# Reordering one turn of an RWKV-6 and mixture-of-depths kernel: ranks, picks, comparison and score sums at other places in the queues

## The chip, the core and the metric

The kernel runs on one core of a Trainium2 chip. The metric is the device time of one execution in microseconds (us). Before the change the median of three runs is 212.65 us (212.56 to 212.82). The profile is one execution with a span of 211.0 us.

Engines in the profile: PE is TensorE (PEld its weight loads), DVE is VectorE, ACT is ScalarE, POOL is GpSimd, SP is the queue that issues the loads and stores. Each engine works through its own queue in order, so an instruction that waits holds up all that stand behind it.

## The reference

First an RWKV-6 recurrence runs over each batch and head, then a mixture-of-depths layer lets the 128 rows of each batch with the highest scores through a feed-forward block. B = 4, H = 8, S = 768, D = 48, C = H x D = 384, F = 1024, capacity = 128.

```python
for t in range(S):
    cur = einsum('bhd,bhe->bhde', u * k[t], v[t])
    y[t] = einsum('bhd,bhde->bhe', r[t], state + cur)
    state = w[t][..., None] * state + einsum('bhd,bhe->bhde', k[t], v[t])
x = y as (B, S, H * D)
scores = x @ w_gate
for b in range(B):
    top = the 128 rows of x[b] with the highest scores
    ye = relu(x[b, top] @ w1) @ w2
    out[b, top] = x[b, top] + sigmoid(scores[b, top])[:, None] * ye
```

All other rows of out are x.

## The kernel before

The sequence is cut into chunks of 128 rows: 6 in each batch, 24 in all, numbered n. Within a chunk the recurrence is made of matrix products. Products of decays from the right and from the left of the chunk scale k and r into K and R; the scores R by K, masked to what lies before (sc, L404), multiply v; the state that comes in adds its share (L437); K with v gives what the chunk adds to the state (kv, L484).

There is no scheduler. The work is put into the queues by hand, in `turn(i)` (L729), which is called for i from -2 to 24. One turn holds work for several chunks, each at another stage:

- chunk i+2: the decays are transposed into PSUM (ps_w, L271) and scanned from the right and the left (L291 and L302 on VectorE); k is transposed too.
- chunk i+1: K and R are made (L349 on VectorE), and the scores R by K (ps_s, L396).
- chunk i: K is turned back to rows (`back`, L278, copied to kt on ScalarE, L414), the mask is applied (sc), v is multiplied with the chunk's own term (rk times u, summed by head on ScalarE in eight instructions of two rows each in the profile, L372; then vo, L381 and L385), kv and the outputs yt follow (L484, L429, L437; yt is copied on ScalarE, L442). L278, L271, L484 are on TensorE. For the first 8 chunks kv is copied aside on ScalarE (kvs, L490); later the state is made from PSUM on VectorE (mid, L503).
- chunk i-1: yt is turned to rows, copied (x, L453 on ScalarE) and completed (L454 on GpSimd), stored; its product with the gate weights is made on GpSimd (scr, L459) and summed on ScalarE into the score (L464).
- chunk i-2: its 128 scores are compared with those of the chunks before it (`others_compared`, L526 on VectorE), transposed so that they stand in every row (ps_e, L536 on TensorE), copied aside (every, L538 on ScalarE) and compared among themselves (`own_compared`, L543 on VectorE).

A chunk that is the last of its batch has no `back` and no kv, so turns 5, 11, 17 and 23 lack these. I cut the profile into turns at the starts of the scan L291; turn i ends where the scan of chunk i+2 starts.

Once a batch has all its comparisons, the generator `mixture(b)` (L554) ranks and fetches its rows: 21 small products with a column of minus ones count how often a row lost (ps_r, L570), VectorE adds that to the other counts (rank, L576 and L577) and makes six pick matrices (L587), products with these give the row numbers (ps_i, L594, then idx, L600), and an indirect DMA on GpSimd's queue gathers the 128 rows (xe, L609). They are transposed (ps_x, L618, copied as xeT, L620), and the gate is computed anew from them (scr_x, L628 on GpSimd, L631 and L632 on ScalarE). The generator is advanced at named places of a turn by `mix(place=...)`: the word that it yields is the place at which it goes on.

The feed-forward block is the generator `forward` (L641): 8 pieces of three products (ps_h, L654, every fourth followed by the copy hid on ScalarE, L659) and 8 pieces of one product (ps_f, L666). Each product in fp32 shows as two rows in the profile. `fed_in_turn` puts some pieces into each turn, at two places. From turn 10 on there is always a batch in this stage.

PSUM tiles come from small pools. The tag "w" has one buffer, which ps_w and ps_e share. The tag "t" has two buffers for the five tiles of a turn (back, yt's rows, r, k and kv). The tag "v" has one, for ps_yt and for the small tiles of `mixture`.

Loads of v, r, w and k for later chunks are issued at the end of each turn (`loads`, L156), with four buffers each.

Of the kernel before, what the change touches and what calls it, by code (L numbers as in the profile page):

```python
# [10 lines left out]
FP32 = mybir.dt.float32  # L11
# [7 lines left out]
L = 128  # L19
# [18 lines left out]
def kernel(  # L38
# [40 lines left out]
    nc = tc.nc  # L79
# [285 lines left out]

    def own_values(t, heads):
        rk = t["rk"]
        if heads[0] == 0:
            t["own"] = lev.tile([L, H], FP32, tag="own", name="own")
        o = t["own"]  # L370
        for h in heads:
            nc.scalar.activation(  # L372
                out=rk[:, h, :], in_=rk[:, h, :], func=AF.Copy, accum_out=o[:, h:h + 1]
            )
# [135 lines left out]

    against = {}

    def others_compared(t):

        b, ci = chunks[t["n"]]
        if ci == 0:
            while len(against) > 1:
                mix()
            against[b] = (
                mod.tile([L, S - L], FP32, name="every", bufs=2),  # L520
                mod.tile([L, NCH, S], BF16, name="ahead", bufs=2),
                lost_bufs[b % 2],
            )
        every, ahead, lost = against[b]
        if ci > 0:
            nc.vector.tensor_scalar(  # L526
                out=ahead[:, ci, 0:ci * L], in0=every[:, 0:ci * L],
                scalar1=score[:, b, ci:ci + 1], scalar2=None,
                op0=ALU.is_ge, op1=ALU.add, accum_out=lost[:, ci, 0:1],
            )  # L530

    def in_all(t):

        b, ci = chunks[t["n"]]
        t["e"] = ps = psW.tile([L, L], FP32, tag="w", name="ps_e")
        nc.tensor.transpose(ps, score[:, b, ci:ci + 1].to_broadcast([L, L]), ident)  # L536
        if ci < NCH - 1:
            nc.scalar.copy(out=against[b][0][:, ci * L:(ci + 1) * L], in_=ps)  # L538

    def own_compared(t):  # L540
        b, ci = chunks[t["n"]]
        ahead, lost = against[b][1:]
        nc.vector.scalar_tensor_tensor(  # L543
            out=ahead[:, ci, ci * L:(ci + 1) * L], in0=t.pop("e"),
            scalar=score[:, b, ci:ci + 1], in1=after_f,
            op0=ALU.is_ge, op1=ALU.mult, accum_out=lost[:, ci, 1:2],
        )

    def compared(t):
        others_compared(t)  # L550
        in_all(t)
        own_compared(t)

    def mixture(b):  # L554

# [12 lines left out]
        for e in range(NCH):  # L568
            for c in range(e + 1):
                nc.tensor.matmul(  # L570
                    ps[:, c:c + 1], ahead[:, e, c * L:(c + 1) * L], minus,
                    start=(e == 0), stop=(e == NCH - 1), skip_group_check=True,
                )
        against.pop(b)
        rank = mod.tile([L, NCH], FP32, name="rank", bufs=2)
        nc.vector.tensor_reduce(out=rank, in_=lost, axis=AX.X, op=ALU.add)  # L576
# [2 lines left out]
        for gi, (c0, n) in enumerate(groups):  # L579
# [6 lines left out]
            for c in range(NCH):  # L586
# [1 line left out]
                    out=pick[:, c, :], in0=slots, scalar1=at[:, c:c + 1], scalar2=None,  # L588
                    op0=ALU.is_equal,
                )  # L590
            yield "half"
            ps = room([L, 2], "ps_i")
            for c in range(NCH):
                nc.tensor.matmul(  # L594
# [31 lines left out]

            scr = mod.tile([L, C], FP32, name="scr_x")
            nc.gpsimd.tensor_mul(scr, xe, wg_bc)  # L628
            yield "half"
            own = mod.tile([L, 1], FP32, name="own", bufs=2)  # L630
            nc.scalar.activation(out=scr, in_=scr, func=AF.Copy, accum_out=own)  # L631
            nc.scalar.activation(out=own, in_=own, func=AF.Exp, scale=-1.0)  # L632
# [55 lines left out]
    def step(f, n, *more):  # L688
        if 0 <= n < N:
            f(work.setdefault(n, dict(n=n)), *more)  # L690
# [38 lines left out]
    def turn(i):  # L729
        soon = i >= N - 1  # L730
        step(first_left, i + 1)
        if i < 1:
            step(scaled_aside, i + 1, "K", "right")
        step(own_products, i + 1)
        step(own_values, i, range(FIRST))
        step(carry, i - 1, work.get(i))
        if i > 0:
            step(scaled, i + 1, "K", "right")
        if i >= 0:
            step(own_weights, i + 1)  # L740
        if soon:
            step(masked, i)
        if i == N - 1:
            sums.extend(check_sums())
        if i < N:
            step(others_compared, i - 2)
        step(back, i)
        mix(place="half")
        if i < N:
            step(in_all, i - 2)  # L750
        if not soon:
            step(masked, i)
        if i < N:
            step(own_compared, i - 2)
        step(rows_out, i - 1, soon)
        step(row_scores_soon if soon else row_products, i - 1)
        step(own_values, i, range(FIRST, H))
        step(own_results, i)
        fed_in_turn(PIECES // 2, 2 if i >= N - 1 else 1)
        step(inputs_t, i + 1, "R", r_bufs)  # L760
        if i == -1:
            spread(wg_bc, wg_row)
        step(scaled, i + 1, "R", "left")
        step(decays_t, i + 2)
        mix(place="mid")
        if i == -2:
            warm(2)
        step(range_check, i + 2)
        if i == -1:
            spread(u_bc.rearrange("p h d -> p (h d)"), u_row)  # L770
            step(own_weights, i + 1)
        step(inputs_t, i + 2, "K", k_bufs)
        if i == -2:
            warm(1)
        step(carry_products, i)
        step(outputs_t, i)
# [107 lines left out]
```

## Time and profile before

Lengths of turns, and the busy time of the engines in them (us):

| turn | stretch | length | PE | DVE | ACT | POOL |
|---|---|---|---|---|---|---|
| 2 | 19.08 to 26.06 | 6.98 | 5.55 | 5.61 | 5.98 | 5.39 |
| 4 | 32.59 to 39.12 | 6.53 | 5.65 | 6.01 | 5.62 | 5.45 |
| 5 | 39.12 to 45.52 | 6.40 | 5.14 | 6.05 | 5.50 | 5.70 |
| 6 | 45.52 to 51.86 | 6.34 | 5.50 | 6.10 | 5.42 | 4.43 |
| 7 | 51.86 to 58.34 | 6.48 | 5.52 | 6.23 | 5.91 | 5.23 |
| 8 | 58.34 to 66.48 | 8.14 | 6.84 | 6.87 | 5.78 | 5.95 |
| 9 | 66.48 to 73.07 | 6.59 | 5.76 | 6.05 | 3.92 | 5.39 |
| 10 | 73.07 to 81.18 | 8.11 | 7.86 | 6.27 | 5.92 | 6.10 |
| 13 | 96.39 to 103.32 | 6.93 | 6.93 | 6.49 | 5.14 | 4.88 |
| 15 | 114.61 to 121.95 | 7.34 | 7.27 | 6.51 | 4.03 | 4.52 |
| 16 | 121.95 to 130.24 | 8.29 | 8.03 | 6.28 | 5.90 | 6.95 |
| 17 | 130.24 to 138.40 | 8.16 | 6.74 | 6.55 | 5.02 | 5.52 |
| 18 | 138.40 to 145.46 | 7.06 | 7.06 | 6.19 | 4.79 | 4.81 |
| 19 | 145.46 to 152.38 | 6.92 | 6.92 | 6.48 | 5.13 | 4.84 |
| 21 | 162.29 to 169.63 | 7.34 | 7.27 | 6.52 | 4.04 | 5.82 |

Turns 8, 14 and 20 rank and pick a batch. Over the whole span TensorE is busy 186.7 us (88%), VectorE 160.3 (76%), ScalarE 128.4 (61%), GpSimd 139.5 (66%).

A row of a timeline is: start, length, engine, line, operation, what it writes and reads, count, and in brackets the idle time before it with what ended that. A busy time adds up instructions that overlap a little, so an engine can be at its limit slightly above or below the length of a stretch; a matmul's end is modelled. Idle time of an engine matters only where that engine, or one that waits for it, sets the end of the turn.

### The profile page before, as it was taken

What the parts mean: (1) busy time and instruction counts of PE and PEld (TensorE: products, weight loads), DVE (VectorE), ACT (ScalarE), POOL (GpSimd) and SP (SyncE); (2) the same over time, 40 slices, a digit from 0 to 9 for tenths busy, and PEclk for the clock granted to TensorE, in tenths of its full rate; (3) what the DMA queues carried; (4) which work ended last, traced back from release to release, by engine and by line L of the source; (5) the groups of instructions that cost most, each with busy time, mean ns of one, the idle gap of its engine ahead of it and who ended that gap; (6) DMA issues with size and microseconds to landing.
All of it is one profiled execution on the core that took longest, in us unless ns stands there. A gap on an engine that the chain in (4) does not pass through costs nothing.

```text
span 211.0 us, 7151 instructions
## 1 busy us (share of the span) xinstructions
PE 186.7 (88%) x2673; PEld 151.8 (72%) x2673; DVE 160.3 (76%) x348; ACT 128.4 (61%) x653; POOL 139.5 (66%) x186
## 2 busy tenths in 40 slices
PE   7988889878898899799969999799988999999980
PEld 3567678766676798698858788689766788786940
DVE  6999799999979987798957887798959885781010
ACT  5478988889874865757444747666744647710300
POOL 8698789886787787569619497596637797301301
PEclk9999999999999999999996999999999999999998
DMA  8999999999998999786693974958651340111101
GB/s 112 164 163 153 182 196 180 242 189 240 197 242 162 223 221 229 166 180 147 129 135 86 142 146 108 164 115 132 132 115 38 78 114 13 67 37 44 37 8 42
DMA packets 105390, 28.86 MB, mean 137 GB/s; under 512 B 100482, under 2 KB 104580, under 8 KB 105348
## 3 DMA queue, kind: packets, MB, share of 16 engines
q1 hardware_dynamic: 104304, 26.65, 69.4%
q0 software_dynamic: 512, 1.57, 2.4%
q8 instruction: 23, 0.38, 0.8%
q14 instruction: 19, 0.16, 0.3%
q10 hardware_dynamic: 532, 0.10, 0.2%
HBM read 22.81 MB, written 5.51 MB: 134 GB/s over the span
## 4 chain that ended last, share of the span: by engine, by line
PE 63%; ACT 13%; DVE 11%; SPq 6%; DMA 3%; issue 3%; POOL 0%; POOLq 0%; ACTq 0%; DVEq 0%
PE ps_f L666 11%; PE ps_yt L429 9%; PE ps_h L654 7%; PE ps_t L271 7%; PE ps_yt L437 6%; PE ps_w L271 6%; PE ps_kv L484 5%; SPq L151 5%; PE ps_s L396 5%; ACT rk L372 4%; DVE sc L404 3%; PE ps_t L278 3%; DMA v_buf<-in_v_dram 3%; ACT scr L464 3%; ACT yt L442 2%
## 5 line engine op out<-in xcount | busy, mean ns | idle before, releaser
L372 ACT ACTIVATE rk<-rk 128x48 f32<-128x48 f32 x192 | 44.5, 239 | 0.0
L454 POOL TENSOR_TENSOR x<-x,vo 128x384 f32<-128x384 f32 x22 | 22.2, 1007 | 27.6 <-ACT x L453 27.5
L442 ACT COPY yt<-ps_yt 128x512 f32<-128x512 f32 x24 | 14.1, 588 | 38.9 <-PE ps_yt L437 35.2
L372 ACT ACTIVATION_READ_ACCUMULATOR rk<-rk 128x1 f32 x192 | 37.6, 196 | 0.0
L302 DVE TENSOR_TENSOR_SCAN left<-ps_w,from_left 128x511 f32<-128x511 f32 x24 | 30.7, 1280 | 0.9
L404 DVE TENSOR_TENSOR sc<-ps_s,before_f 128x1024 f32<-128x1024 f32 x24 | 29.3, 1219 | 2.2 <-PE ps_s L396 2.2
L291 DVE TENSOR_TENSOR_SCAN right_buf<-ps_w,from_right 128x511 f32<-128x511 f32 x24 | 29.2, 1216 | 2.3 <-PE ps_w L271 1.0
L396 PE MATMUL ps_s<-R,K 64*64 64x128 f32 x768 | 26.4, 271 | 0.0
L429 PE MATMUL ps_yt<-sc,v_buf 128*64 128x128 f32 x384 | 25.6, 275 | 0.0
L654 PE MATMUL ps_h<-xeT,w 128*128 128x128 f32 x192 | 25.6, 280 | 0.0
L364 POOL TENSOR_TENSOR rk<-rk,u_bc 128x384 f32<-128x384 f32 x24 | 24.0, 1001 | 0.9 <-DVE right_buf L291 0.4
L666 PE MATMUL ps_f<-w,hid 128*128 128x384 f32 x64 | 24.5, 511 | 0.0
L654 PEld LDWEIGHTS ps_h<-xeT,w 128*128 128x128 f32 x192 | 22.9, 192 | 1.9 <-issue 1.4
L361 POOL TENSOR_TENSOR rk<-r_buf,k_buf 128x384 f32<-128x384 f32 x24 | 24.1, 1005 | 0.1
L459 POOL TENSOR_TENSOR scr<-x,wg_bc 128x384 f32<-128x384 f32 x22 | 22.1, 1004 | 1.7
L396 PEld LDWEIGHTS ps_s<-R,K 64*64 64x64 f32 x768 | 22.2, 133 | 1.3 <-issue 1.0
L429 PEld LDWEIGHTS ps_yt<-sc,v_buf 128*64 128x64 f32 x384 | 20.6, 137 | 0.6 <-issue 0.5
L271 PE MATMUL ps_t<-ident,r_buf 128*128 128x128 f32 x96 | 15.5, 285 | 5.2 <-ACT kt L414 4.6
L349 DVE TENSOR_TENSOR R<-ps_t,left 128x512 f32<-128x512 f32 x24 | 16.5, 689 | 4.6 <-PE ps_t L271 3.4
L271 PE MATMUL ps_w<-ident,w_buf 128*128 128x128 f32 x96 | 16.2, 294 | 3.7 <-DVE ahead L543 3.4
L381 POOL TENSOR_TENSOR vo<-v_buf,own 128x384 f32<-128x384 f32 (+1 forms) x24 | 17.7, 736 | 2.0 <-ACT rk L372 2.0
L271 PEld LDWEIGHTS ps_t<-ident,r_buf 128*128 128x128 f32 x96 | 11.2, 145 | 9.2 <-ACT kt L414 6.7
(118 smaller groups left out, 359.6 us busy)
## 6 DMA issues: line engine op xcount, KB each, us to landing
k_buf<-in_k_dram SPq DMA_DIRECT2D x24, 192.0 KB, 4.7
r_buf<-in_r_dram SPq DMA_DIRECT2D x24, 192.0 KB, 5.0
v_buf<-in_v_dram SPq DMA_DIRECT2D x24, 192.0 KB, 4.5
out_dram<-x SPq DMA_DIRECT2D x24, 192.0 KB, 2.1
w_buf<-in_w_dram SPq DMA_DIRECT2D x23, 192.0 KB, 5.4
w<-in_moe_w_dram SPq DMA_DIRECT2D x3, 512.0 KB, 6.3
w<-in_moe_w_dram SPq DMA_DIRECT2D x4, 384.0 KB, 4.7
w_buf<-in_w_dram ACTq DMA_DIRECT2D x1, 96.0 KB, 3.3
```

The lines of the kernel that those rows point to most:

```text
L271: nc.tensor.transpose(ps[:, j, :], src(j), ident)
L291: nc.vector.tensor_tensor_scan(out=flat[:, W - 2::-1], data0=wt[:, W - 1:0:-1], data1=from_right.rearrange("p j t -> p (j t)")[:, W - 2::- ...
L302: nc.vector.tensor_tensor_scan(out=left.rearrange("p j t -> p (j t)")[:, 1:W], data0=wt[:, 0:W - 1], data1=start.rearrange("p j t -> p (j ...
L361: nc.gpsimd.tensor_mul(rk, r_bufs[n % NBUF][:, :, 0:D], k_bufs[n % NBUF][:, :, 0:D])
L364: nc.gpsimd.tensor_mul(t["rk"], t["rk"], u_bc)
L372: nc.scalar.activation(out=rk[:, h, :], in_=rk[:, h, :], func=AF.Copy, accum_out=o[:, h:h + 1])
L396: nc.tensor.matmul(ps[half(c), q, j, :], t["K"][half(q), j, half(c)], t["R"][half(q), j, :], start=True, stop=True,)
L404: nc.vector.tensor_mul(t["sc"].rearrange("p q j t -> p (q j) t"), ps.rearrange("p q j t -> p (q j) t"), _heads(before_f, 2 * HP),)
L429: nc.tensor.matmul(ps[half(c), j % 2, j // 2, :], vt[:, 2 * j + q, :], t["sc"][:, q, j, :], start=(j < 2), stop=(old is None), skip_group_ ...
L454: nc.gpsimd.tensor_add(xj, xj, vo)
L654: nc.tensor.matmul(ps[:, q, :], w1[:, dc, (f0 + q) * L:(f0 + q + 1) * L], xeT[:, dc, :], start=(dc == 0), stop=(dc == NDC - 1),)
L666: nc.tensor.matmul(ps, hid[:, fc, :], w2[:, fc, :], start=(fc == 0), stop=(fc == NFC - 1))
```

## The change

It moves work within the queues and leaves every instruction as it is:

- `own_values`: in turns without feed-forward work (up to turn 9) all eight heads are summed on ScalarE behind x; before, five of them stood in front of kt. Later turns keep five and three.
- `compared` becomes one step, in front of the mask: transpose, comparison with the others, own comparison, then the copy `every`. Before, the mask stood in front of the own comparison, and the copy in front of it too.
- `row_sums`, the sum that makes the score, moves in front of kvs and yt on ScalarE; it stood behind them and behind hid.
- The rank products move in front of the second group of feed-forward pieces of the turn, by a place of their own ("ranks").
- Rank and picks on VectorE move behind mid and K ("picks").
- The products of the picks, idx and the gather, and in a later turn the gate's sum and exponential, move to a place behind the turn's first group of feed-forward pieces ("late"); so the gather stands behind the turn's L454, L459 and L381 on GpSimd.

It is meant to let instructions that others wait for pass those that nobody waits for at that moment.

```diff
     def own_values(t, heads):
         rk = t["rk"]
-        if heads[0] == 0:
+        if "own" not in t:
             t["own"] = lev.tile([L, H], FP32, tag="own", name="own")
...
-    def others_compared(t):
+    def compared(t):
...
+        own = score[:, b, ci:ci + 1]
+        lo, hi = ci * L, (ci + 1) * L
+
+        ps = psW.tile([L, L], FP32, tag="w", name="ps_e")
+        nc.tensor.transpose(ps, own.to_broadcast([L, L]), ident)
         if ci > 0:
             nc.vector.tensor_scalar(
-                out=ahead[:, ci, 0:ci * L], in0=every[:, 0:ci * L],
-                scalar1=score[:, b, ci:ci + 1], scalar2=None,
+                out=ahead[:, ci, 0:lo], in0=every[:, 0:lo], scalar1=own, scalar2=None,
                 op0=ALU.is_ge, op1=ALU.add, accum_out=lost[:, ci, 0:1],
             )
...
+        nc.vector.scalar_tensor_tensor(
+            out=ahead[:, ci, lo:hi], in0=ps, scalar=own, in1=after_f,
+            op0=ALU.is_ge, op1=ALU.mult, accum_out=lost[:, ci, 1:2],
+        )
         if ci < NCH - 1:
-            nc.scalar.copy(out=against[b][0][:, ci * L:(ci + 1) * L], in_=ps)
...
+            nc.scalar.copy(out=every[:, lo:hi], in_=ps)
...
+        yield "picks"
         against.pop(b)
         rank = mod.tile([L, NCH], FP32, name="rank", bufs=2)
...
-            yield "half"
+            yield "late"
             ps = room([L, 2], "ps_i")
...
             nc.gpsimd.tensor_mul(scr, xe, wg_bc)
-            yield "half"
+            yield "late"
             own = mod.tile([L, 1], FP32, name="own", bufs=2)
...
         step(own_products, i + 1)
-        step(own_values, i, range(FIRST))
+
+        first = FIRST if feed or picked else 0
+        step(own_values, i, range(first))
         step(carry, i - 1, work.get(i))
         if i > 0:
             step(scaled, i + 1, "K", "right")
+        mix(place="picks")
...
+        step(back, i)
         if i < N:
-            step(others_compared, i - 2)
-        step(back, i)
-        mix(place="half")
-        if i < N:
-            step(in_all, i - 2)
+            step(compared, i - 2)
         if not soon:
             step(masked, i)
-        if i < N:
-            step(own_compared, i - 2)
         step(rows_out, i - 1, soon)
         step(row_scores_soon if soon else row_products, i - 1)
-        step(own_values, i, range(FIRST, H))
+        step(own_values, i, range(first, H))
         step(own_results, i)
         fed_in_turn(PIECES // 2, 2 if i >= N - 1 else 1)
+        mix(place="late")
...
         step(range_check, i + 2)
+        if not soon:
+            step(row_sums, i - 1)
...
         step(scores, i + 1)
+        if 0 <= i - 2 < N - 1 and chunks[i - 2][1] == NCH - 1:
+            mixing.append([mixture(chunks[i - 2][0]), "ranks"])
+        mix(place="ranks")
         fed_in_turn(PIECES - PIECES // 2, 1 if i == N - 1 else 0)
         if i == N - 1:
             step(compared, i - 1)
-        if not soon:
-            step(row_sums, i - 1)
         step(scans, i + 2)
-        if 0 <= i - 2 < N - 1 and chunks[i - 2][1] == NCH - 1:
-            mixing.append([mixture(chunks[i - 2][0]), "end"])
         mix(place="end")
...
-        mixing.append([mixture(B - 1), "half"])
+        mixing.append([mixture(B - 1), "picks"])
         step(compared, N - 1)
         fed(1)
-        mix()
+        mix(2)
```

More of the change, by code (lines that the diff above doesn't have):

```diff
@@ L524, in others_compared @@
         every, ahead, lost = against[b]
+        own = score[:, b, ci:ci + 1]
+        lo, hi = ci * L, (ci + 1) * L
+        ps = psW.tile([L, L], FP32, tag="w", name="ps_e")
+        nc.tensor.transpose(ps, own.to_broadcast([L, L]), ident)
         if ci > 0:
             nc.vector.tensor_scalar(
-                out=ahead[:, ci, 0:ci * L], in0=every[:, 0:ci * L],
-                scalar1=score[:, b, ci:ci + 1], scalar2=None,
+                out=ahead[:, ci, 0:lo], in0=every[:, 0:lo], scalar1=own, scalar2=None,
                 op0=ALU.is_ge, op1=ALU.add, accum_out=lost[:, ci, 0:1],
             )
[L532 to L542, printed above, removed]
         nc.vector.scalar_tensor_tensor(
-            out=ahead[:, ci, ci * L:(ci + 1) * L], in0=t.pop("e"),
-            scalar=score[:, b, ci:ci + 1], in1=after_f,
+            out=ahead[:, ci, lo:hi], in0=ps, scalar=own, in1=after_f,
             op0=ALU.is_ge, op1=ALU.mult, accum_out=lost[:, ci, 1:2],
         )
[L549 to L552, printed above, removed]
+        if ci < NCH - 1:
+            nc.scalar.copy(out=every[:, lo:hi], in_=ps)
     def mixture(b):
```

## The prediction

> **What bounds the kernel now.** I read the page's chain first. TensorE carries most of it, yet no engine carries it throughout:
>
> ```profile
> PE 63%; ACT 13%; DVE 11%; SPq 6%; DMA 3%; issue 3%; POOL 0%; POOLq 0%; ACTq 0%; DVEq 0%
> ```
>
> So I cut the span into turns, each from one start of the scan L291 to the next (turn i ends with the scan of chunk i+2), and asked for the busy time of each stretch:
>
> ```profile
> 26.06:32.59 6.53, 5.65 (x104) 4.77 (x102) 5.87 (x12) 5.63 (x32) 5.45 (x8) 1.00 1.05 194
> 81.18:89.33 8.15, 6.73 (x111) 5.79 (x110) 6.54 (x14) 5.02 (x26) 5.52 (x7) 1.00 0.85 202
> 89.33:96.39 7.06, 7.06 (x107) 6.54 (x105) 6.19 (x11) 4.79 (x27) 4.82 (x7) 1.00 0.78 175
> 103.32:114.61 11.29, 9.67 (x134) 7.77 (x133) 7.29 (x20) 4.75 (x26) 6.81 (x8) 0.85 0.60 107
> 152.38:162.29 9.91, 8.22 (x134) 6.48 (x133) 7.30 (x20) 4.75 (x26) 5.50 (x7) 1.00 0.29 62
> ```
>
> Columns after the length: PE, PEld, DVE, ACT, POOL busy, granted clock, DMA share, GB/s. Turn 3 (first line) has no full engine: it is a loop of waits. Turn 11 has 1.4 us in which TensorE does nothing. Turn 12 is full of TensorE. Turns 14 and 20 rank a batch; TensorE idles 1.6 to 1.7 us in each, and in turn 14 its clock falls to 0.85. The chain in order of time gives the loop of turn 3, then turn 11, then turn 14:
>
> ```profile
> 28.55 0.59 ACT yt L442
> 29.13 0.52 ACT scr L464 x2
> 29.73 0.86 ACT rk L372 x8
> 31.29 0.66 PE ps_t L271 x4
> ...
> 84.53 0.88 PE ps_h L654 x6
> 85.43 0.60 ACT hid L659
> 86.03 0.51 ACT scr L464 x2
> 86.56 0.62 DVE ahead L526 x2
> 87.18 1.14 DVE sc L404
> 88.64 0.66 PE ps_w L271 x4
> ...
> 106.47 1.49 PE ps_f L666 x4
> 107.96 0.52 PE ps_r L570 x21
> 108.70 1.06 DVE pick L587 x6
> 110.09 0.60 PE ps_t L278 x4
> ```
>
> In turn 3 kt (the timeline has it at 30.78) stands on ScalarE behind scr and five heads of rk. In turn 11 scr stands behind hid, so the comparison, the mask and at last the decays' transposes (ps_w) wait for it. In turn 14 VectorE waits 2.18 us for ps_r, which stands behind ps_f, and TensorE then waits 1.6 us for mid, which stands behind the picks. The list of waits says what else holds ps_w:
>
> ```profile
> DVE ahead L543 <- ACT every L538: 6.7, 11, 1.4
> PEld ps_w L271 <- DVE ahead L543: 5.6, 9, 1.1
> DVE rank L577 <- PE ps_r L570: 5.5, 4, 2.2
> ```
>
> **What the Trainium skill says.** "PSUM — Partial Sum Buffer", section "PSUM bank collisions raise a hardware error", says that no two engines may touch one bank and quadrant at once, two reads included, so software must order them. The first wait above is such an order: L543 and the copy L538 only read ps_e. The change turns it round: the copy then waits for L543. The same page, "Engine vs sequencer instructions", calls the queues of ScalarE and VectorE strict FIFO, as the chain of turn 3 shows. "TensorE: Matmul & The Clock Gate", section "What's actually happening", has a clock that falls with a lack of recent work; turn 14 agrees (0.85, and four transposes in 1.06 us at 112.81 against 0.60), though its gap of 1.6 us is shorter than the page's window. "DMA: Bandwidth & Descriptors", section "Anatomy of one DMA — SWDGE (gpsimd) path", gives about 2 us fixed; the row gathers here take 3.1 us to land (median), 4.9 us in turn 8.
>
> **The change part by part.** No instruction is added or taken away; all is order. Durations are starts of neighbours in dense stretches of the timeline.
>
> *Plain turns 2 to 9: all eight heads of rk behind x, and scr in front of kvs and yt.* ScalarE's loop from yt to kt loses 0.52 (scr) and 5 x 0.227 = 1.14 us (rk). Both go into time in which ScalarE idled for yt (0.9 us in turn 3) or worked without anyone waiting. ScalarE's sum is yt 0.48, left 0.08, kt 0.36, every 0.15, x 0.37, rk 1.82, vo 0.91, junk 0.60, scr 0.52, kvs 0.22 = 5.51 us, so it no longer sets the turn. Behind the moved rk stand vo and, on GpSimd, L381, needed only next turn. The next limit is VectorE: scan 1.26, alls 0.19, reciprocal 0.22, left 1.20, K 0.58, own comparison 0.27, mask 1.14, R 0.60 = 5.46 us, and the others' comparison 0.27, 0.40, 0.53, 0.66, 0.79 for chunks 1 to 5. But the built order adds a wait: back's transposes now take the PSUM buffer that K frees (they waited for ScalarE before). K ends 3.45 us into the turn; back 0.39, ps_e 0.27 and handoffs of about 0.2 put the own comparison at 4.3, and 0.27 + 1.14 + 0.60 end the turn at 6.3. Turns 3 to 7 become 6.3, 6.3, 6.0 (no back), 6.15, 6.3 instead of 6.53, 6.53, 6.40, 6.34, 6.48: 1.2 us. Turn 2: ps_e ends at 23.55, so the mask runs from 23.9 and the scan starts at 25.7, not 26.06: 0.4. Together **1.6 us**. The loads do not stop this: v lands 2.9 us ahead of its use in turn 3 (29.44 against 32.35) and 3.6 us ahead in turn 5.
>
> *Turn 8: K in front of the picks.* K to 3.45, reduce 0.14, ps_r done near 4.0, sum to 4.2, picks 1.0, own comparison 0.27, mask 1.14, index 0.15, R 0.60: 7.35 instead of 8.14, **0.8 us**.
>
> *Gather later.* It now stands behind L381 on GpSimd. In turn 8 x's copy ends at about 6.1, L454 and L459 to 8.2, L381 to 9.05; landed after 3.1 to 4.9 us, that is 12.2 to 14.0. TensorE wants the rows 5.4 us into turn 9, at 12.75. So turn 9 loses between 0 and 1.2 us; I take **-0.2 us**. For batches 1 and 2 the rows land 2.7 us before their use: nothing.
>
> *Gate's sums late.* In turns 10 and 16 scr_x and its exponential (0.76 us) leave the place in front of every. ps_w waited 0.49 and 0.26 us for that; TensorE takes it up: **0.4 and 0.3 us**.
>
> *Turns 11 and 17: score early.* The product L459 ended at 82.6, so scr runs in front of yt. ps_e then follows ps_h at once. On TensorE from the end of ps_h (84.9 after the shift of turn 10): ps_e 0.25, yt's transposes 0.4, ps_h 0.9, R's transposes 0.45, ps_w 0.55 = 87.45; on VectorE own comparison to 85.5, mask to 86.6, R 86.95 to 87.55. The scan starts at 87.55, or 88.05 without the shift, against 89.33: **1.3 us each**.
>
> *Turns 14 and 20: ranks in front of ps_f, mid and K in front of the picks.* TensorE from the end of ps_s at 106.47: ps_r 0.52, ps_f 1.49, back 0.5, ps_e 0.27, yt 0.45, ps_f 0.75, picks' products 0.25, R 0.5, ps_w 0.6 = 111.8. VectorE: rank and picks end at about 108.6, hidden under ps_f; own comparison 109.3 to 109.6, mask 110.75, index 110.95, R 111.85. With handoffs the scan starts at about 112.2 instead of 114.61: **2.4 us**, the clock's fall included. Turn 20 from 155.54 by the same sum: 160.8 instead of 162.29, **1.5 us**.
>
> *Mask behind the own comparison (all feed turns).* The mask now waits for ps_e, behind up to 1.53 us of ps_h. Turn 12: ps_e ends at 94.24, comparison 94.6, mask 95.75, R 96.35; before, R ran 95.79 to 96.48. Turn 13: R at 102.6 against 102.71. Turn 21: 169.07 against 169.04. TensorE fills that time with yt's transposes, ps_h or ps_f, R and ps_w, so turns 12, 13, 15, 18, 19, 21 change by **0**. Turn 22: scr ends at about 179.4 and yt stands behind it, **-0.1**. The tail after the last turn keeps its order.
>
> Sum: 1.6 + 0.8 - 0.2 + 0.4 + 1.3 + 2.4 + 0.3 + 1.3 + 1.5 - 0.1 = 9.3 us; 212.65 - 9.3 = 203.3.
>
> **Rivals.** *Deeper* (12%): plain turns reach VectorE's sums without the detour over back (1.1 us more) and the gather lands in time; with small gains in full turns 2.1 us more: 201.2. *Partial* (23%): ScalarE and GpSimd (5.5 us each in 6.3) stay coupled and only turns 8, 11, 14, 17, 20 gain, 7.3 us, less 0.5 for the gather: 205.9. For it: those busy sums. *Given back* (15%): on top, the late mask costs 0.3 us in the eight other feed turns: 208.3; the margins of turns 12, 13 and 21 are 0.1 us. *Slower* (5%): the mask, in turn 10 moved from 77.56 to 79.1, holds R and ps_kv by 0.5 us in eleven turns (+5.5), gathers come 0.4 us late three times (+1.2), turns 11 and 17 gain nothing, and only 8, 14 and 20 pay (-4.7): 214.6. Against it: 2.2 us of TensorE work follow ps_e in those turns.
>
> **Numbers.** My forecast has 45%. The range 200.8 to 207.8 leaves out part of the deeper case, about half of the given-back one and the slower one. Faster 0.93, same 0.02, slower 0.05.
>
> **What would show it.** Turns 14 and 20 near 8.9 and 8.4 us with VectorE's wait for ps_r gone; turns 11 and 17 near 6.9; turns 3 to 7 between 6.0 and 6.3 with ps_w no longer waiting for L543; turn 12 unchanged at 7.06; a wait of ps_x for the gather in turn 9. Wrong if turns 12, 13, 18 and 19 grow, or if the plain turns stay at 6.5.

## The result and the profile after

| kernel | median us | range | ratio to before, 95% interval |
|---|---|---|---|
| before, beside it | 212.61 | 211.56 to 212.82 | 1 |
| changed | 205.2 | 204.5 to 207.49 | 0.968 [0.9598, 0.9762] |

The change makes the kernel 3.2% faster, by 7.4 us. The forecast was 203.3 us (200.8 to 207.8), so the direction is right, the time lies inside the range, and 1.9 us of the gain are missing. The profiled execution has a span of 203.4 us against 211.0, and these 7.6 us can be laid out turn by turn (lengths in us; each gain is the difference to before):

| turns | before | gain forecast | after | gain measured |
|---|---|---|---|---|
| 2 to 7 | 39.26 | 1.6 | 37.53 | 1.73 |
| 8 | 8.14 | 0.8 | 8.00 | 0.14 |
| 9 and 10 | 14.70 | 0.2 (0.4 less 0.2) | 16.13 | -1.43 |
| 11 and 17 | 16.31 | 2.6 | 13.60 | 2.71 |
| 12, 13, 18, 19 | 27.97 | 0 | 27.98 | -0.01 |
| 14 | 11.29 | 2.4 | 8.06 | 3.23 |
| 15 and 21 | 14.68 | 0 | 16.10 | -1.42 |
| 16 | 8.29 | 0.3 | 7.83 | 0.46 |
| 20 | 9.91 | 1.5 | 8.06 | 1.85 |
| start, 22 and the rest | 60.45 | -0.1 | 60.11 | 0.34 |
| sum | 211.0 | 9.3 | 203.4 | 7.6 |

So the reordering of scores, ranks and picks gave all that was forecast and more, and three places gave less: turn 8, turns 9 and 10, and turns 15 and 21. The profile's chain of work by engine shows where the loss in turns 9 and 10 comes from; DMA had 3% of it before:

```profile
PE 57%; DMA 11%; DVE 11%; ACT 8%; SPq 6%; issue 3%; POOL 2%; POOLq 0%; DVEq 0%
```

The busy time by stretch, columns as before (length, PE, PEld, DVE, ACT, POOL, granted clock, DMA share, GB/s), for turns 3, 11, 12, 14 and 20, and for turn 10:

```profile
25.45:31.78 6.33, 5.64 (x101) 4.78 (x101) 5.68 (x12) 5.70 (x32) 5.48 (x8) 1.00 1.10 207
80.67:87.47 6.80, 6.61 (x110) 5.68 (x109) 6.46 (x15) 4.80 (x26) 4.54 (x6) 1.00 1.05 222
87.47:94.56 7.09, 7.09 (x107) 6.51 (x105) 6.18 (x13) 5.45 (x30) 5.44 (x6) 1.00 0.97 190
101.46:109.52 8.06, 8.06 (x136) 6.56 (x134) 7.59 (x21) 4.80 (x25) 5.20 (x7) 1.00 0.67 126
146.31:154.37 8.06, 8.06 (x136) 6.55 (x134) 7.59 (x21) 4.68 (x25) 5.10 (x6) 1.00 0.38 78
70.54:80.67 10.13, 8.17 (x126) 7.59 (x126) 6.28 (x13) 6.47 (x36) 6.79 (x8) 1.00 1.03 224
```

TensorE is now busy for the whole of turns 14 and 20, at full clock. Turn 10 has 2 us in which TensorE does nothing. The chain in order of time says what it waits for, and what stands ahead of that; the last lines are turn 14, where ps_f follows ps_r without a gap:

```profile
65.55 0.52 POOL vo L381
66.07 0.48 issue
66.55 5.91 DMA xe<-out_dram,idx
72.50 0.55 PE ps_x L607 x3
...
104.62 0.61 PE ps_r L558 x21
105.23 1.40 PE ps_f L655 x4
```

The list of waits (who, for whom: total us, times, longest):

```profile
DVE ahead L535 <- PE ps_e L529: 13.3, 15, 2.9
ACT every L540 <- DVE ahead L535: 5.3, 6, 1.3
PEld ps_x L607 <- DMA xe<-out_dram,idx: 3.4, 2, 2.7
```

The waits of VectorE for ps_r (5.5 us) and of ps_w for L543 (5.6 us) are no longer among the long ones. New are the own comparison's wait for ps_e, and ps_x's for the gathered rows: 2.7 us for batch 0 and 0.7 us for batch 1.

### The profile page after: what moved, and what is told of

It reads as the page before. It is cut to its first block, busy times and chain, and to the rows that moved or that the text cites. A ratio compares the mean times of both kernels' runs of the same rounds, so it can differ in the third digit from the quotient of the medians.

```text
span 203.4 us, 7181 instructions
## 1 busy us (share of the span) xinstructions
PE 184.8 (91%) x2673; PEld 151.2 (74%) x2673; DVE 160.2 (79%) x348; ACT 129.8 (64%) x653; POOL 139.4 (69%) x186
## 4 chain that ended last, share of the span: by engine, by line
PE 57%; DMA 11%; DVE 11%; ACT 8%; SPq 6%; issue 3%; POOL 2%; POOLq 0%; DVEq 0%
PE ps_h L643 11%; PE ps_f L655 10%; PE ps_s L396 6%; PE ps_yt L429 6%; DMA xe<-out_dram,idx 6%; SPq L151 6%; PE ps_t L278 6%; PE ps_t L271 5%; PE ps_kv L484 4%; PE ps_yt L437 3%; DMA v_buf<-in_v_dram 3%; DMA r_buf<-in_r_dram 2%; PE ps_w L271 2%; DVE sc L404 2%; ACT rk L372 2%
## 5 line engine op out<-in xcount | busy, mean ns | idle before, releaser
L372 ACT ACTIVATE rk<-rk 128x48 f32<-128x48 f32 x192 | 44.0, 236 | 0.0
L454 POOL TENSOR_TENSOR x<-x,vo 128x384 f32<-128x384 f32 x22 | 22.1, 1005 | 25.8 <-ACT x L453 25.7
L372 ACT ACTIVATION_READ_ACCUMULATOR rk<-rk 128x1 f32 x192 | 37.0, 193 | 0.0
L655 PE MATMUL ps_f<-w,hid 128*128 128x384 f32 x64 | 23.8, 499 | 0.2 <-issue 0.2
L459 POOL TENSOR_TENSOR scr<-x,wg_bc 128x384 f32<-128x384 f32 x22 | 22.1, 1003 | 1.7
L442 ACT COPY yt<-ps_yt 128x512 f32<-128x512 f32 x24 | 13.9, 581 | 11.5 <-PE ps_yt L437 10.7
L381 POOL TENSOR_TENSOR vo<-v_buf,own 128x384 f32<-128x384 f32 (+1 forms) x24 | 17.7, 737 | 3.4 <-ACT rk L372 3.4
L414 ACT COPY kt<-ps_t 128x384 f32<-128x384 f32 x20 | 9.6, 478 | 14.8 <-PE ps_t L278 14.8
L535 DVE SCALAR_TENSOR_TENSOR ahead<-ps_e,score,after_f 128x128 bf16<-128x128 f32 x24 | 8.4, 349 | 13.4 <-PE ps_e L529 13.3
L484 PEld LDWEIGHTS ps_kv<-v_buf,kt 128*64 128x64 f32 x320 | 11.0, 137 | 7.4 <-DVE R L349 6.9
```

The costliest lines, as they stand in the source:

```text
L372: nc.scalar.activation(out=rk[:, h, :], in_=rk[:, h, :], func=AF.Copy, accum_out=o[:, h:h + 1])
L454: nc.gpsimd.tensor_add(xj, xj, vo)
L459: nc.gpsimd.tensor_mul(t["scr"], t.pop("x"), wg_bc)
L655: nc.tensor.matmul(ps, hid[:, fc, :], w2[:, fc, :], start=(fc == 0), stop=(fc == NFC - 1))
```

## The experiments

All times are medians with the ratio to the kernel before that ran beside them; turn lengths come from each kernel's profile. My theory after this reading was: the gather is the main loss, since it is issued behind L381 and then lands late. The rival was that VectorE's new order (picks, comparison, late mask) loses the time and that any earlier gather would only uncover that.

### The gather in front of the rows again

```diff
             for c in range(NCH):
                 nc.vector.tensor_scalar(out=pick[:, c, :], ...)
-            yield "late"
+            yield "half"
...
+        mix(place="half")
         step(rows_out, i - 1, soon)
```

> The changed kernel with one thing moved: the picks' products, the index and the gather stand in front of the rows of x again (behind the mask), so the gather passes L454, L459 and L381 on GpSimd. Theory: the 1.9 us by which the changed kernel (205.2) misses the forecast is mostly the gather behind those three, 2.5 us later. Then the gather of batch 0 is issued near 64.0 us instead of 66.55, lands before 70.0, ps_x has no wait (2.7 us now), turn 10 falls from 10.13 to about 7.5 us, turn 15 by 0.3: 202.3 us, between 201.8 and 203.0. Rival: the time is lost in the order of VectorE (picks, late mask), and another wait takes the gather's place in turns 9 and 10: above 204.5.

Measured: 202.92 us (201.99 to 203.14), ratio 0.9559 [0.951, 0.9609]. The gather is issued at 64.37 and lands after 4.6 us, at 68.97; ps_x has no wait. Turn 10 takes 8.04 us instead of 10.13, and turn 16 takes 7.39 instead of 7.83. The time fell by 2.3 us, near what the theory had (202.3 us), although turn 10 did not reach 7.5. What the rival expected did not show up. One thing was not expected: turn 9 took 7.12 us instead of 6.00, with a clock of 0.85. The two lines are turns 9 and 10.

```profile
64.64:71.76 7.12, 7.05 (x108) 6.16 (x106) 6.02 (x14) 4.79 (x27) 7.00 (x8) 0.85 0.98 226
71.76:79.80 8.04, 7.66 (x122) 6.96 (x120) 6.17 (x13) 6.38 (x36) 6.25 (x8) 1.00 1.10 212
```

### The loads behind it, not in front of it

Does the gather land late because of its place on GpSimd, or because of what runs beside it? This kernel keeps the place and moves the turn's loads.

```diff
         mix(place="mid")
+        if i in (9, 15, 21):
+            loads(i + 4)
...
-        if i > -2:
+        if i > -2 and i not in (8, 14, 20):
             loads(i + 5)
```

> The changed kernel with the gather where the change put it, but the loads of v, r, w and k at the end of turns 8, 14 and 20 are issued later, behind ps_x of the next turn. Theory A: the gather lands 5.9 us after its issue instead of 3.1 because it shares the DMA engines with these loads; without them it lands within 4 us, ps_x waits under 0.9 us instead of 2.7, and the time is 203.0 us (202.5 to 203.8). Theory B: the landing is a matter of the gather itself or of its place on GpSimd; it stays above 5 us, ps_x waits 2.3 us or more, and the time stays at 205.2.

Measured: 203.82 us (202.46 to 205.35), ratio 0.9606 [0.9547, 0.9666]. The two theories split by batch. For batch 1 the landing fell from 5.75 to 3.3 us, its wait is gone, and turns 15 and 16 together take 15.11 us instead of 16.00 (15.94 in the second profile of the changed kernel, below). For batch 0 the landing stayed at 5.9 us, and ps_x waited 1.8 us. The queue that issues the loads (start, length of the issue) explains why, the gather being issued at 66.64:

```profile
61.87 2.94 SPq L151 DMA_DIRECT2D w_buf<-in_w_dram  x1
64.90 1.19 SPq L151 DMA_DIRECT2D k_buf<-in_k_dram  x1
66.14 1.06 SPq L183 DMA_DIRECT2D w<-in_moe_w_dram  x1
```

These loads stand at the end of turn 7, at 56.6 us. The issue of a load of w takes 1.1 us in the median of this kernel and 2.9 us here, and the DMA share is between 0.91 and 1.17 in turns 2 to 11: the queue is behind by half a turn and more. The loads that my edit moved are issued only from 68.16 us on in the changed kernel, 1.6 us behind the gather, so for batch 0 the edit took away the wrong ones.

### The same, with weight loads moved as well

```diff
-    WEIGHT_TURNS = list(range(2, 2 * NDC + 2, 2)) + list(range(2 * NDC + 1, 100))
+    WEIGHT_TURNS = list(range(2, 2 * NDC + 2, 2)) + list(range(2 * NDC + 3, 100))
```

> loads_late with one thing more: the two weight loads of 384 KB of turns 7 and 8 are issued two turns later. In loads_late the gathers of batches 1 and 2 landed in 3.3 and 3.1 us instead of 5.75 and 3.6, but that of batch 0 still in 5.9, and the queue SP was then still issuing loads of the turn before (w, k, weights, up to 67.3 us, the gather at 66.6). Theory: it is this backlog on DMA engines that are full up to turn 11; without the weights it is worked off sooner, the gather of batch 0 lands within 4.5 us, ps_x waits under 0.5 us instead of 1.8, and the time is 202.5 us (201.5 to 203.4). Rival: the first gather takes near 5.9 us whatever runs beside it; the wait stays, 203.8 us.

Beside the edit of the last kernel, this one moves all four weight loads of 384 KB by two turns, so that none is left in turns 7 and 8.

Measured: 202.27 us (201.72 to 202.68), ratio 0.953 [0.9489, 0.9572]. The gather of batch 0, still issued behind L381 at 66.57, lands after 3.4 us:

```profile
DMA to landing us min/median/max: 3.4/3.4/3.4
```

ps_x waits 0.2 us, turn 9 takes 5.99 us and turn 10 takes 8.04. The busy share of the DMA engines in the changed kernel and in this one, over the same 6.1 us from 66.5 us on (each digit is a fortieth of that, in tenths), shows the difference: there they are busy until the rows have landed at 72.46, here they have nothing left to do from 69.6 on.

```profile
DMA  1387999985599897996886987999899999999999
DMA  9999999999975994564300000000000000402899
```

So the cause is not the place on GpSimd alone, but that place together with DMA engines that are still working off a backlog. The slow landing by itself goes with the backlog and not with the place: in three of the kernels below that have the gather at its early place (the heads, the score's sum and the comparisons alone) it took 5.8 us to land in turn 8, and there ps_x did not wait for it. "DMA: Bandwidth & Descriptors" of the Trainium skill, section "Queues, rings and completion order", says that each DMA engine takes turns between the queues that have work for it, packet by packet. The runs agree in so far as the landing grows with what the loads' queue still has to move, from 3.4 to 5.9 us at the same time of issue; the taking of turns itself is not shown here. The gather's bytes are not the reason: 3.1 us is the landing of batch 3's gather, with the same 128 rows. Whether the weight loads alone would do it was not tried.

### The mask in front of the comparisons again

```diff
+        if not soon:
+            step(masked, i)
         if i < N:
             step(compared, i - 2)
-        if not soon:
-            step(masked, i)
```

> The changed kernel with the mask in front of the comparisons again, all else as changed. Theory: the late mask costs in turns 15 and 21, where VectorE has mask, ye and R behind ps_e, 0.6 us each (8.17 and 7.93 go to about 7.5 and 7.35), and in the plain turns 3 and 4, where VectorE waits for ps_e before the mask, up to 0.4 us each: 203.5 us (202.8 to 204.2). Rival: the order is what made the plain turns faster, since the copy every and with it the copy of x come 1.2 us later when the own comparison stands behind the mask; turns 2 to 7 go back by 0.1 to 0.3 us each, which eats the gain: 204.8 to 206.

Measured: 208.86 us (208.31 to 210.2), ratio 0.9866 [0.9812, 0.992], so 3.7 us slower than the changed kernel in the first comparison. The theory's part holds: turns 15 and 21 both fell to 7.10 us. But it is outweighed. Turns 2 to 7 lose 1.24 us together (turns 5 and 6 went back from 5.97 and 6.11 to 6.51 and 6.64), turn 8 loses 0.34, and turns 11 and 17 lose 0.23 each: 2.0 us. The rival was right in this. That the time lies above the 206 us it named is partly the clock, which was at 0.78 in turn 9 (7.76 us instead of 6.00; ps_kv and ps_yt's first half took 3.0 us instead of 1.7), and partly the gather. It is issued 0.7 to 0.8 us later in its turn, ps_x waits 1.6 us for it in turn 10 and 2.0 in turn 16 (0.7 in the changed kernel), and turn 16 takes 9.65 us instead of 7.83. The rival's mechanism stands in the list of waits:

```profile
ACT every L540 <- DVE ahead L535: 12.1, 13, 2.3
PEld ps_w L271 <- ACT every L540: 6.5, 11, 1.2
DVE R L349 <- ACT x L453: 6.4, 8, 1.2
```

The own comparison runs behind the mask, the copy every waits for the comparison, x waits in ScalarE's queue behind every, and ps_w and R wait for these two. In the kernel before the mask was first too, but every did not wait for the comparison, and turns 5 to 7 took 19.22 us together against 19.63 here; that this wait is the whole difference is my reading.

### The product of rk with u behind the picks

In turn 8 the six picks took 1.65 us instead of the forecast's 1.0. The timeline of the changed kernel has a GpSimd product beside them:

```profile
60.62 1.00 POOL L364 TENSOR_TENSOR rk<-rk,u_bc 128x384 f32<-128x384 f32 x1
60.84 1.32 DVE L576 TENSOR_SCALAR pick<-slots,rank 128x128 bf16<-128x128 bf16 x4
```

and the instructions on the tile pick (min/median/max in ns) have one far off the others:

```profile
L576 DVE TENSOR_SCALAR pick<-slots,rank x24: 241/244/833, 60.8 to 181.4; 128x128 bf16<-128x128 bf16 x24
```

The first pick starts at 60.84 and lasts 0.83 us, to 61.67; the product ends at 61.62.

```diff
+        picking = mixing and mixing[0][1] == "picks"
         mix(place="picks")
-        if i >= 0:
+        if i >= 0 and not picking:
             step(own_weights, i + 1)
...
         mix(place="late")
+        if i >= 0 and picking:
+            step(own_weights, i + 1)
```

> The changed kernel with the product of rk with u (L364 on GpSimd) moved behind the gather in turns 8, 14 and 20, so that it no longer runs while VectorE makes the picks. Theory: the first pick of turns 8 and 14 took 0.83 and 0.61 us instead of 0.24 because it could not start its access before GpSimd's product was over; without it all 24 picks take 0.24 to 0.26 us, and turn 8 falls from 8.00 to about 7.4 us. In turns 14 and 20 TensorE is full, so they stay at 8.06. Time 204.6 us (204.2 to 205.0). Rival: the long pick is a start-up cost of the first pick behind the rank; it stays, and the time is 205.2.

Measured: 203.23 us (202.48 to 205.66), ratio 0.959 [0.9525, 0.9655]; better than expected. All picks are short again and turn 8 takes 7.43 us, as expected:

```profile
L576 DVE TENSOR_SCALAR pick<-slots,rank x24: 244/249/255, 60.9 to 179.5; 128x128 bf16<-128x128 bf16 x24
```

"SBUF — State Buffer" of the Trainium skill, section "Who interferes with whom", has VectorE's two-port forms, which tensor_scalar can take, share one pair of ports with GpSimd: whichever was first holds it for its whole instruction. The trace agrees: the pick ends 0.05 us behind the product that started first. What the time gains beyond 204.6 lies mostly in turns 9 and 10 (15.32 us instead of 16.13): the gather was issued 0.5 us sooner and here landed in 5.1 us.

### Each part alone, on the kernel before

Heads of rk behind x:

```diff
-        step(own_values, i, range(FIRST))
+        first = FIRST if feed or picked else 0
+        step(own_values, i, range(first))
...
```

> The kernel before with the first edit alone: all eight heads of rk behind x up to turn 9. If ScalarE's loop from yt to kt set the plain turns, as the forecast said, taking 1.14 us out of it shortens turns 3, 4, 6 and 7, by 0.2 to 0.4 us each (turn 5 has no kt and moves less), and nothing else moves: 211.2 us (210.4 to 212.0). Rival: the limit is VectorE's detour (own comparison behind the mask, ps_w behind the comparison); then the turns keep 6.3 to 6.5 us and the time is 212.4 or more.

Measured: 210.36 us (208.73 to 213.29), ratio 0.9911 [0.9875, 0.9946]. Turns 2, 3 and 4 gain 0.72, 0.29 and 0.22 us, turn 9 gains 0.38; turns 5 to 7 gain nothing. So of the turns 2 to 7 the loop over ScalarE was the limit in 2 to 4 only.

The score's sum in front of kvs and yt:

```diff
         step(range_check, i + 2)
+        if not soon:
+            step(row_sums, i - 1)
...
-        if not soon:
-            step(row_sums, i - 1)
```

> The kernel before with the score's sum alone in front of kvs and yt. Forecast: turns 11 and 17 go from 8.15 to about 6.9 us each, 2.6 us, and the plain turns 3 to 7 gain up to 0.3 us each, since 0.52 us leave the loop from yt to kt: 209.3 us (208.5 to 210.1). Rival: yt waits for the sum where GpSimd delivers scr late, and gives back half of it: 211 or more.

Measured: 209.31 us (207.95 to 212.21), ratio 0.9876 [0.9793, 0.9959]. Turns 11 and 17 take 7.35 us, a gain of 0.80 each and not 1.3; turns 2 to 5 gain 0.55, 0.52, 0.45 and 0.20 us, and turn 9 gains 0.38. That the time meets the forecast of 209.3 is luck: the parts of the sum differ, and no execution took that time (three took 207.95 to 208.13 us, three 210.48 to 212.21).

The comparisons in one step in front of the mask:

```diff
-        if i < N:
-            step(others_compared, i - 2)
         step(back, i)
         mix(place="half")
         if i < N:
-            step(in_all, i - 2)
+            step(compared, i - 2)
         if not soon:
             step(masked, i)
-        if i < N:
-            step(own_compared, i - 2)
...
```

> The kernel before with the comparisons in one step in front of the mask, and the copy every behind the own comparison, nothing else changed. Theory: in the plain turns this order takes the mask (1.14 us) out of the way from K to every and to the copy of x, and it is what keeps them short (the changed kernel with the mask in front again took 208.9 instead of 205.2). Then turns 2 to 9 gain 0.1 to 0.3 us each, and turns 15 and 21 lose 0.6 us each, with ye and R behind the late mask: 212.0 us (211.2 to 212.8). Rival: in this kernel ScalarE's loop with five heads still sets the plain turns, they stay as they are, and only the losses remain: 213.8 us.

Measured: 209.8 us (207.88 to 211.22), ratio 0.9887 [0.9851, 0.9923]; a larger gain than either theory had. Turns 5, 6 and 7 gain 0.37, 0.23 and 0.25 us, turns 2 to 4 under 0.1 each. Turns 10, 11, 17, 12 and 18, for which I had expected nothing, gain 0.42, 0.36, 0.37, 0.18 and 0.18. Turn 16 takes 7.40 us, against 7.86 in each of the other three kernels of this section (the 8.29 of before holds a pause in ps_s, 1.47 us instead of 1.05, that they don't have). Turns 15 and 21 lose 0.37 each (7.71 us), less than the 0.6 expected. Turns 8 and 9 gain 0.36 and 0.16. That a late mask costs only where little work stands behind ps_e on TensorE is my reading; no run isolates it.

Ranks in front of ps_f, rank and picks behind mid and K:

```diff
         if i > 0:
             step(scaled, i + 1, "K", "right")
+        mix(place="picks")
...
         step(scores, i + 1)
+        if 0 <= i - 2 < N - 1 and chunks[i - 2][1] == NCH - 1:
+            mixing.append([mixture(chunks[i - 2][0]), "ranks"])
+        mix(place="ranks")
...
```

> The kernel before with the rank products in front of the second pieces and rank and picks behind mid and K, and the gather still in front of the rows of x. Forecast: turn 14 from 11.29 to 8.0 to 8.9 us, turn 20 from 9.91 to 8.0 to 8.4, turn 8 from 8.14 to 7.4 to 8.0 (the first pick waits 0.6 us while GpSimd multiplies rk by u): 207.5 us (206.5 to 208.5). Rival: what is gained before the picks is paid behind them, since idx now stands in front of the mask on VectorE and waits for the picks' products: 209.5 or more.

Measured: 206.91 us (206.61 to 208.28), ratio 0.9804 [0.9745, 0.9863]. Turns 14 and 20 take 8.23 us each, turn 8 takes 7.91; the rival's wait of idx for the picks' products is 0.3 us at most. In turn 8 the first pick starts at 62.26 us, just as GpSimd's product with u ends, so the wait that I had expected there did not come. This part alone gives 5.3 us, more than any other.

The gains of the four parts are not shares of the whole: they add up to 12.3 us, and the change has 7.4. They meet at the same waits. In the plain turns 2 to 4 the whole even gains less than a part: 1.23 us with the heads alone, 1.52 with the score's sum alone, and 0.93 with the whole change. There the changed kernel has back's transposes and ps_e between K and the mask; but the kernel with the mask in front, above, gains no more (0.90 us), so which part of the change costs this is open.

The four kernels also separate the clock from the queues. Without the ranks' move, turns 14 and 20 take either 9.9 us or 11.3 to 11.5; turn 14 and turn 20 of the kernel with the score's sum alone:

```profile
100.27:110.19 9.92, 8.22 (x134) 6.48 (x133) 7.31 (x20) 4.83 (x25) 5.49 (x7) 1.00 0.56 102
146.73:158.04 11.31, 9.69 (x134) 7.78 (x133) 7.23 (x21) 4.83 (x26) 6.82 (x8) 0.85 0.32 72
```

The same work, with 1.6 to 1.7 us in which TensorE is idle, costs 1.4 us more where the clock falls. The profile of before had that fall in turn 14 only. With the ranks moved, both turns are at 8.23 and at full clock:

```profile
102.80:111.03 8.23, 8.16 (x134) 6.49 (x133) 7.66 (x21) 4.79 (x25) 5.93 (x7) 1.00 0.66 128
148.38:156.61 8.23, 8.16 (x134) 6.50 (x133) 7.66 (x20) 4.79 (x25) 5.93 (x7) 1.00 0.38 80
```

### The changed kernel again, and what can be had beyond it

These three ran on one chip, beside the kernel with the weight loads moved. The first is the changed kernel without an edit.

> The changed kernel unaltered, on the same chip as the next three, to compare with. Theory: 205.2 us again (204.5 to 207.5); ps_x waits for the gather of batch 0 for more than 2 us. Rival: that wait was an accident of one execution; then the gather lands within 4 us here and the time is below 203.5.

Measured: 205.0 us (203.76 to 207.44), ratio 0.9664 [0.9612, 0.9715]. The gather of batch 0 landed in 5.0 us here, later than the rival had it, and ps_x waited 1.3 us, less than the 2 us I had expected; turn 9 had a clock of 0.90 and took 6.75 us. So 9 and 10 together took 15.16 us. The wait is no accident, but its size changes with the landing.

The second joins two edits, the gather in front and the product behind the picks.

> The changed kernel with the gather in front of the rows of x (as in gather_early, 202.9) and the product of rk with u behind the picks (as in weights_late, where turn 8 took 7.43 us instead of 8.00). Theory: the two are separate causes and add up: turn 8 at 7.4, no wait of ps_x, turns 9 and 10 together at 14.1 to 15.2: 202.1 us (201.0 to 202.6). Rival: the gain of the picks in turn 8 was an earlier gather only, and the two don't add up: 202.9.

Measured: 202.06 us (201.93 to 202.23), ratio 0.952 [0.9481, 0.9558]. Turn 8 takes 7.42 us, turns 9 and 10 together 14.44 us. The causes add up: 2.9 us are gained on the changed kernel beside it, and apart they gave 2.3 (the gather) and 0.6 (turn 8). The spread over the executions is 0.3 us, against 2.5 for the changed kernel on the same chip.

The third adds the mask first in two turns:

```diff
+        last = i in (15, 21)
+        if last:
+            step(masked, i)
         if i < N:
             step(compared, i - 2)
-        if not soon:
+        if not (soon or last):
             step(masked, i)
```

> both_early with the mask in front of the comparisons in turns 15 and 21 alone, where ps_f stands in front of ps_e and ye behind the mask. Theory: in these two turns VectorE runs mask, ye and R behind the own comparison and sets the end; with the mask first they fall from 7.7 to about 7.1 us each, as in mask_front (7.10), and no other turn changes: 201.0 us (200.0 to 201.8), faster than both kernels. Rival: what turns 15 and 21 gain is lost in 16 and 22, and the time is that of both_early.

Measured: 202.19 us (201.84 to 202.46), ratio 0.9524 [0.9485, 0.9563]: no gain over the second. Turn 15 takes 7.57 us and turn 21 takes 7.72, not 7.1, and turn 16 gives the 0.15 us back. The theory's limit is gone in turn 21, VectorE has ye done by 157.4, but another has taken its place:

```profile
154.97 1.01 POOL L364 TENSOR_TENSOR rk<-rk,u_bc 128x384 f32<-128x384 f32 x1
157.66 0.66 PE L271 MATMUL ps_t<-ident,r_buf 128*128 128x128 f32 x4 [0.84 <-ACT kt L414]
```

From turn 10 on five heads of rk stand in front of kt on ScalarE. With the gather in front and then the product of rk with u behind the rows of x on GpSimd, that product ends only near 156.0, and the heads, kt and r's transposes follow it. To move the product in turn 8 alone, where all eight heads stand behind x, with the mask first in turns 15 and 21, was not tried.

So three versions (these two and the one with the weight loads moved) are faster than both kernels, at 202.1 to 202.3 us, 1.3 to 1.4% under the changed kernel beside them.

## Why the prediction was right, and where it was off

The direction and most of the mechanisms were right. That the time lies as near as 1.9 us to the forecast is partly luck: misses of 3.7 us one way stand against 2.0 the other way, as the last paragraph of this section adds up.

**Plain turns 2 to 7 (1.6, measured 1.73): right.** 6.33, 6.34, 5.97, 6.11 and 6.34 us were measured for the 6.3, 6.3, 6.0, 6.15 and 6.3 of the text. The account over K, back, ps_e, own comparison, mask and R is what the timeline of turns 3 and 4 shows (the own comparison waits 0.55 us for ps_e in turn 3); in turns 5 to 7 VectorE itself is busy for all but 0.1 us. ps_w no longer waits for the own comparison. The shares were less clear than the text had them: the gains come from ScalarE's loop in turns 2 to 4, and from the new order of the comparisons in 5 to 7.

**Turn 8 (0.8, measured 0.14): a term was mis-sized.** The step "picks 1.0" rested on the picks of before. Moved behind K, they meet GpSimd's product with u, and the first pick takes 0.83 us. Without that meeting the turn takes 7.43 us; the text had 7.35.

**Gather later (-0.2): the mechanism was right, the size was off.** The wait of ps_x appeared where it was promised. But the text had L381 done 9.05 us into turn 8 and the gather issued then; it was issued at 10.0 (66.55 less 56.54), of which the slow picks made 0.6 (9.4 without them). And I took the landing as 3.1 to 4.9 us, which is what before had at its earlier place; it was 5.9. With the backlog removed, turns 9 and 10 take 14.03 us, with it 16.13 (15.16 in the second profile): this term is 1.1 to 2.1 us and not 0.2. For batch 1, where the text has "nothing", it is 0.4 to 0.8 us more: turn 16 takes 7.39 to 7.40 us with an early landing and 7.83 or 8.23 with the late one. The DMA share of 1.05 in turn 3 and 0.85 in turn 11 was in my first table, and I used it for nothing.

**Turns 10 and 16, gate's sums (0.4 and 0.3): the gain came, but hardly from them.** Without the gather's wait, turns 9 and 10 take 14.03 us and turn 16 takes 7.40. The new order of the comparisons alone, with the gate's sums where they were, has 14.13 and 7.40. They were not moved alone, but these runs leave about 0.1 us for them. (The 0.46 us of the table for turn 16 is measured from the 8.29 of before, with its pause in ps_s.)

**Turns 11 and 17 (1.3 each, measured 1.35 and 1.36): right in sum, not in its reason.** The score's sum alone gives 0.80. The new order of the comparisons gives 0.36 by itself, and 0.2 us come only with both. The text gave the whole to the sum.

**Turns 14 and 20 (2.4 and 1.5, measured 3.23 and 1.85): right.** VectorE's wait for ps_r is gone, and both turns are shorter than the 8.9 and 8.4 of the text, because TensorE is busy for their full 8.06 us, without the handoffs that the text allowed for. 1.4 us of the 3.23 is the clock's fall. For turn 20 the text's sum is off: it says "by the same sum", but leaves out the 0.4 us of handoffs that it gave turn 14. With them it comes to 161.3 and a gain of 1.0 us, so the 1.5 was nearer to the 1.85 by a slip.

**Mask behind the own comparison (0 in turns 12, 13, 15, 18, 19, 21): right in four turns, wrong in 15 and 21.** "Turn 21: 169.07 against 169.04" left out an instruction that stands between mask and R there, ye. VectorE in turn 21 of the changed kernel:

```profile
159.77 0.35 DVE L535 SCALAR_TENSOR_TENSOR ahead<-ps_e,score,after_f 128x128 bf16<-128x128 f32 x1 [1.35 <-PE ps_e L529]
...
160.04 1.22 DVE L404 TENSOR_TENSOR sc<-ps_s,before_f 128x1024 f32<-128x1024 f32 x1
161.18 0.61 DVE L662 SCALAR_TENSOR_TENSOR ye<-ps_f,gate,xe 128x384 f32<-128x384 f32 x1
161.70 0.68 DVE L349 TENSOR_TENSOR R<-ps_t,left 128x512 f32<-128x512 f32 x1
```

r's transposes had ended at 160.85, so R runs late by VectorE's queue alone, for ye stands in front of it with 0.52 us. With it the text's own sum gives 0.56 us more. In the second profile of the changed kernel both turns take 7.71 us, 0.37 more than before. The other 0.68 us of the table appear only in the first profile: ps_s took 1.51 us there instead of 1.05 in turn 15, and TensorE's row PEld paused 0.39 us ahead of ps_f in turn 21, instead of 0.17. Why is not known.

By the profiles 1.7 us of the forecast gain are missing: 1.63 in turns 9 and 10 (the gather), 0.66 in turn 8 (the picks) and 1.42 in turns 15 and 21, against 1.18 more than forecast in turns 14 and 20 and 0.83 more in the other lines. Of the rivals, the partial case (205.9) came nearest in time, but not for its reason: the plain turns did gain.

## What to carry to other kernels

Before you move a gather or another wanted transfer back in a queue, look at what the DMA engines are doing at the new time of issue, and price its landing from there, not from its old place. When you let one instruction pass another, write down the whole queue between the new place and the next instruction that somebody waits for, once for each kind of turn. An order that loses in two turns can still win in ten, so judge a part both by a version that undoes it alone and by one that has it alone.

## What the runs showed of the hardware that was not expected

A pick of 0.24 us on VectorE (bf16, 128x128) took 0.83 us beside a GpSimd product of 1.00 us that had started 0.22 us earlier, and ended with it. The gather of batch 0 took 4.2 to 6.3 us to land in thirteen of the fourteen profiles, beside loads, and 3.4 us in the one with the weight loads moved; the gathers with no load beside them took 3.0 to 3.3 us. While the loads were behind, the issue of one load of w held SyncE's queue for 2.9 us, against a median of 1.1.

The clock of TensorE fell to 0.85 in turn 14 or turn 20 in some profiles and not in others, with the same instructions and gaps (9.92 against 11.3 us), and to 0.78 to 0.90 in turn 9 in four of the profiles (7.12 us instead of 6.00 in one). What decides between the two was not found. Of the eight such turns with a gap (turns 14 and 20 of before and of the kernels with the heads, the score's sum or the comparisons alone) three show the fall; of the twenty in the ten profiles with the ranks in front of ps_f, none does.

The times of single executions go with these falls. The 43 executions of the kernel before that ran beside the four parts stand in four groups: 210.3 to 210.6 us at a mean granted clock of 0.996 to 0.999, 211.7 to 212.3 at 0.983 to 0.990, 212.8 to 213.4 at 0.980 to 0.982, and 214.3 to 214.4 at 0.973 to 0.975. The profile of before, with one turn of fallen clock, has 0.989. So its median of 212.6 us holds one or two such falls. By an estimate from these groups (210.5 us with none), about 2 of the 7.4 us that the change gains are falls that no longer happen, and the rest is order.
